# Where a reloaded tile lands, and two more places for x, in an adaLN attention and token-mixing kernel

## The chip, the cores and the metric

The kernel runs on one core of one Trainium2 chip. The metric is the device time of one execution in microseconds (us); lower is better. The kernel before was run three times: 2290.21, 2290.84 and 2291.17 us, median 2290.84. The profile is one further execution of it, which took 2293.52 us.

## The reference, cut to what matters

```
mod = (silu(c) @ w_mod)            # six rows: sa, ca, ga, sb, cb, gb
h = layernorm(x) * (1 + ca) + sa
x = x + ga * attention(h)          # 32 heads, 4 segments with a memory between them, then @ wo
h = layernorm(x) * (1 + cb) + sb
# token mixing: layernorm(h) once more, then two products across the 2048 tokens
u = gelu(einsum("bsd,sf->bdf", layernorm(h), w1) + b1)
x = x + gb * (einsum("bdf,fs->bds", u, w2) + b2).transpose
```

x has 2048 tokens of 1024 channels. The change lies between attention and mixing: the product with wo, the sum with x, and the two norms that follow.

## The kernel before, in words

The 2048 tokens are 16 tiles of 128. Attention runs over pieces (a group of four heads, a segment of 512 tokens) and writes its transposed output to oT in DRAM. The stage behind it, the one that the change touches, goes through the 16 token tiles in the order 0, 1, 8, 2, 9, 3, 10, 4, 11, 5, 12, 6, 13, 7, 14, 15. The mixing works on pairs (k, 8 + k): seven combinations of the halves of two tiles are its seven right operands, and its seven products q of a unit replace eight.

For each tile `product` does the following. L714 loads the attention output into otr. L122 and L125 (the helper `split`) make of it the two parts of ots on ScalarE and VectorE. L718 loads x into a tile x1. L729 runs 48 matmuls, 24 for each half of the channels, into two PSUM banks. L732, on VectorE, adds each half to x1 and leaves the bank free. L734 stores x1 to x1d in DRAM, where the end of the kernel needs it.

Then come three steps. `modulated`: the square of x1 on ScalarE (L703, L705, L706) with small VectorE steps (L707 to L709), and L754 and L755, which write the modulated norm into a tile h2; L754 is the last to read x1. `normed`: the square of h2 (L703 again, this time with mb), and L762, the second norm in place. `paired`, for the tiles from 8 on: L688 to L691 make the combinations. Pairs 0 to 2 are split into the operands bA on the spot; the others go to hcd in DRAM (L777 to L779) and come back later (L858).

The places: x1 has two, h2 has three, ots two, otr one. A place goes to the next tile of its name when all that read the last one are done. Tiles 2 and 3 are the EARLY ones: their products run just behind tile 1, while attention still works, since their tokens are complete by then. Their x1 is only stored; when their turn comes, `out_proj` takes a place of x1 again and reloads it from x1d (L744).

The mixing's first weights come by L803 in `prepare`, into a tile wr of 8 KB a partition, of which there are two places; s1, sp and bB are its other operands. Their memory is freed by the last product, wr's already by attention. In the kernel before, both places of wr are loaded when the stage begins.

All DMAs are issued by SyncE's queue (SPq), in one order. That order and the order on each engine come from the framework's scheduler, which takes the program's order for priority and a model of the times for what is ready; in the trace each engine, and SPq, goes through its own list in that order, so an instruction that waits stands before those behind it.

Of the kernel before, what the change touches and what calls it, by code (L numbers as in the profile page):

```python
# [2 lines left out]

# [4 lines left out]
F32 = mybir.dt.float32  # L8
# [9 lines left out]
S, D, H, DH, F = 2048, 1024, 32, 32, 3584  # L18
P = 128
# [27 lines left out]
def attention_and_mlp(ctx, tc, x, wq, wkv, wo, beta, w1, b1, w2, b2, c, wm_a, wm_b, out):  # L47
    nc = tc.nc
    V, A, G, T, SY = nc.vector, nc.scalar, nc.gpsimd, nc.tensor, nc.sync
# [4 lines left out]
    x1d = dram.tile([NT, P, D], F32, name="x1d")  # L54
# [12 lines left out]
    a = par.__enter__()  # L67
# [9 lines left out]
    def bank(tag, bufs, name):  # L77
        return psum.tile([P, 512], F32, tag=tag, bufs=bufs, name=name)
# [39 lines left out]
    def split(dst, src, hi_eng, lo_eng):  # L118

        hi, lo = dst[:, 0], dst[:, 1]  # L120
        if hi_eng is A:
            A.copy(hi, src)  # L122
        else:
            hi_eng.tensor_copy(hi, src)
        lo_eng.tensor_tensor(lo, src, hi.bitcast(F32), op=ALU.subtract)  # L125
# [177 lines left out]
    b = late.__enter__()  # L303
# [263 lines left out]
    def spread(dst, i):  # L567
        SY.dma_start(dst, bass.AP(tensor=modd.tensor, offset=modd.offset + D * i, ap=[[0, P], [1, D]]))
# [45 lines left out]
    for g in range(2, NG):  # L614
        n = 8 * g - 13
# [5 lines left out]
    for j in range(32):  # L621
        n = ML0 + MLS * j
        later(n, lambda j=j: mod_fetch(j), n + 2, lambda r, j=j: mod_late(j, r), "V")
    plan(WO0 - 3, lambda: spread(gaw, 0))
    for i in range(8):
        n = WO0 + WOS * i
# [30 lines left out]
    for q in skp + [late, prj, paw]:  # L657
# [6 lines left out]
    b3, raws, sx = (ctx.enter_context(tc.tile_pool(name=n, bufs=1, side="right", reuse_waits="tile"))  # L664
                    for n in ("b3", "wr", "s1"))
    cw_pool = tc.tile_pool(name="cw", bufs=1, side="right", reuse_waits="tile")
    w = cw_pool.__enter__()
# [18 lines left out]
    def t_combos(E, b11, b12, b21, b22, t):  # L686

        E.tensor_tensor(t[:, 0], b12, b11, op=ALU.subtract)  # L688
        E.tensor_tensor(t[:, 1], b22, t[:, 0], op=ALU.subtract)
        E.tensor_tensor(b12, b22, b12, op=ALU.subtract)  # L690
        E.tensor_tensor(t[:, 2], b21, t[:, 1], op=ALU.subtract)  # L691
# [7 lines left out]
    def rstd(src, nm, mv, sq):  # L699

        if sq is None:
            sq = wq_.tile([P, D], BF16, tag="sq", bufs=1, name="sq")
        A.activation(sq, src, AF.Square, bias=nm, accum_out=mv[:, 2:3])  # L703
        v, r0, t = mv[:, 0:1], mv[:, 1:2], mv[:, 2:3]
        A.activation(r0, t, AF.Ln, scale=1.0 / D, bias=eps)  # L705
        A.activation(r0, r0, AF.Exp, scale=-0.5)  # L706
        V.tensor_scalar(v, t, -0.5 / D, -0.5 * EPS, op0=ALU.mult, op1=ALU.add)  # L707
        V.tensor_scalar(t, v, r0, r0, op0=ALU.mult, op1=ALU.mult)
        V.tensor_scalar(r0, t, 1.5, r0, op0=ALU.add, op1=ALU.mult)  # L709

    def product(tt):

        r = wr_.tile([P, NK, P], F32, tag="otr", bufs=1, name=f"otr{tt}")
        SY.dma_start(r, oT[:, :, P * tt:P * tt + P].rearrange("g p n -> p g n"))  # L714
        os_ = ws_.tile([P, 2, D], F32R, tag="ots", bufs=2, name=f"ots{tt}")
        split(os_, r.rearrange("p a b -> p (a b)"), A, V)
        x1 = w.tile([P, D], F32, tag="x1", bufs=2, name=f"x1_{tt}")
        SY.dma_start(x1, x[P * tt:P * tt + P])  # L718
        ma = w.tile([P, 8], F32, tag="ma", bufs=2 + len(EARLY), name=f"ma{tt}")
        if tt == 0:  # L720
            for i in range(1, 3):
                gm[i] = w.tile([P, D], F32, name=f"gm{i}")
                spread(gm[i], i)
        for nh in range(2):
            ps = bank("pj", 2, f"po{tt}_{nh}")
            n = 0
            for ct in range(NK):
                for i, j in ((0, 0), (0, 1), (1, 0)):
                    T.matmul(ps, os_[:, i, P * ct:P * ct + P], wop[ct, nh][:, j], start=(n == 0), stop=(n == 3 * NK - 1))  # L729
                    n += 1  # L730
            c0, c1 = 512 * nh, 512 * nh + 512
            V.scalar_tensor_tensor(x1[:, c0:c1], ps, 1.0, x1[:, c0:c1], op0=ALU.mult, op1=ALU.add,  # L732
                                   accum_out=ma[:, 5 + nh:6 + nh])
        SY.dma_start(x1d[tt], x1)  # L734
        return x1, ma

    done = {}

    def out_proj(tt):

        if tt in done:
            ma = done[tt]
            x1 = w.tile([P, D], F32, tag="x1", bufs=2, name=f"x1r_{tt}")
            SY.dma_start(x1, x1d[tt])  # L744
        else:
            x1, ma = product(tt)
        h2 = w.tile([P, D], F32, tag="h2", bufs=3, name=f"h2_{tt}")
        mb = w.tile([P, 8], F32, tag="mb", bufs=2, name=f"mb{tt}")

        def modulated():  # L750
            nm = ma[:, 4:5]
            V.tensor_scalar(nm, ma[:, 5:6], ma[:, 6:7], -1.0 / D, op0=ALU.add, op1=ALU.mult)
            rstd(x1, nm, ma, h2 if tt == 15 else None)
            V.scalar_tensor_tensor(h2, x1, nm, gm[2], op0=ALU.add, op1=ALU.mult)  # L754
            V.scalar_tensor_tensor(h2, h2, ma[:, 1:2], gm[1], op0=ALU.mult, op1=ALU.add, accum_out=mb[:, 5:6])  # L755

        def normed():
            nm = mb[:, 4:5]
            V.tensor_scalar_mul(nm, mb[:, 5:6], -1.0 / D)
            rstd(h2, nm, mb, x1 if tt == 15 else None)  # L760
            V.tensor_scalar_mul(mb[:, 3:4], nm, mb[:, 1:2])
            A.activation(h2, h2, AF.Identity, scale=mb[:, 1:2], bias=mb[:, 3:4])  # L762

        def paired():
            if tt < 8:
                pair_h[tt] = h2
                return
            k = tt - 8
            first = pair_h.pop(k)
            t = w.tile([P, 3, 512], F32, tag="tc", bufs=1, name=f"tc{k}")  # L770
            t_combos(G if k == 7 else V, first[:, 0:512], first[:, 512:], h2[:, 0:512], h2[:, 512:], t)
            if k < 3:
                src = [first[:, 0:512], t[:, 0], t[:, 1], h2[:, 0:512], first[:, 512:], h2[:, 512:], t[:, 2]]
                for q in range(NPR):
                    split(bA[q][:, k], src[q], A, V)
            else:
                SY.dma_start(hcd[k, :, 0:2], first.rearrange("p (a n) -> p a n", a=2))  # L777
                SY.dma_start(hcd[k, :, 2:4], h2.rearrange("p (a n) -> p a n", a=2))
                SY.dma_start(hcd[k, :, 4:7], t)  # L779

        return modulated, normed, paired

    for tt in [0] + [i for k in range(1, 8) for i in (k, 7 + k)] + [15]:
        rest = out_proj(tt)
        if tt < 15:
            for f in rest:
                f()
        if tt == 1:
            for i in EARLY:
                done[i] = product(i)[1]  # L790
# [256 lines left out]
```

## Time and profile before

| | |
|---|---|
| median of 3 runs | 2290.84 us (2290.21 to 2291.17) |
| profiled execution | 2293.52 us |
| its span, first to last instruction | 2291.70 us |
| TensorE matmul, busy | 2214.7 us, 97% |
| VectorE, busy | 1677.2 us, 73% |
| ScalarE, busy | 1148.1 us, 50% |
| mean granted TensorE clock | 0.988 |

The span is 1.82 us less than the profiled execution's own time: that is what lies around it. Times inside the profile are us from the span's start. In the timeline a row gives start, length, engine, line, operation, output<-input and count, and in brackets the idle time before it with what ended it. In the list of waits a row gives who waited for whom, the sum in us, how often, and the longest. PE is TensorE, DVE VectorE, ACT ScalarE, POOL GpSimd, SPq SyncE's queue. The names x and h in the profile stand for x1 and h2 here (numbers are left out of names).

### The profile page before, as it was taken

The page shows a single profiled execution, that of the slowest core. Times are in us where ns is not written, and L with a number is a line of the kernel's source. Part 1 is how long each engine was busy: PE and PEld are TensorE (multiplying, and loading weights), DVE is VectorE, ACT ScalarE, POOL GpSimd, SP SyncE. Part 2 cuts the span into 40 slices and gives each one's busy share as a digit, 9 for nine tenths or more (in the row PEclk, how much of TensorE's full clock was granted, in tenths as well). Part 3 has the DMA queues.
Part 4 walks back from the last instruction along what each step waited for, and adds up shares of the span by engine and source line. Part 5 has one row for each costly group of instructions (what it writes and reads, how often), then busy time and mean ns, then how long its engine had stood idle before and what let it go on. Part 6 is the DMA issues. An engine that isn't in the chain of part 4 may idle for free.

```text
span 2291.7 us, 38412 instructions
## 1 busy us (share of the span) xinstructions
PE 2214.7 (97%) x13802; PEld 1903.6 (83%) x13802; DVE 1677.2 (73%) x3798; ACT 1148.1 (50%) x2090; POOL 733.1 (32%) x843
## 2 busy tenths in 40 slices
PE   7999999999999999999799999999999999999999
PEld 6888898888988889987687888888887888888887
DVE  6686677766776777664768565698889787878787
ACT  6476677664665666655555333443334242424232
POOL 5165566564766766644001000023333000000000
PEclk9999999999999999999999999999999999999999
DMA  6656565686566566673366664566557441414133
GB/s 258 201 169 180 144 198 162 180 280 218 165 192 207 169 196 182 202 250 107 114 218 243 238 238 164 192 230 237 207 202 264 173 152 55 152 56 143 55 120 147
DMA packets 172882, 415.72 MB, mean 181 GB/s; under 512 B 17268, under 2 KB 71572, under 8 KB 163732
## 3 DMA queue, kind: packets, MB, share of 16 engines
q1 hardware_dynamic: 172692, 413.27, 54.7%
q8 instruction: 110, 1.80, 0.3%
q14 instruction: 80, 0.66, 0.1%
HBM read 237.28 MB, written 125.06 MB: 158 GB/s over the span
## 4 chain that ended last, share of the span: by engine, by line
PE 77%; DVE 8%; DMA 6%; ACT 3%; POOL 3%; issue 2%; SPq 0%; DVEq 0%; ACTq 0%; POOLq 0%
PE mx L843 42%; PE nps L195 12%; PE qps L203 7%; PE po L729 4%; PE pv L503 3%; POOL ph L489 1%; PE a L474 1%; PE sx L439 1%; DVE ac L850 1%; PE sz L439 1%; DMA x<-in_x_dram 1%; DMA sk<-nt 1%; DVE sp L125 1%; PE rd L411 1%; PE a L477 1%
## 5 line engine op out<-in xcount | busy, mean ns | idle before, releaser
L843 PE MATMUL mx<-bU,sp 128*128 128x512 f32 x2352 | 535.8, 389 | 3.6 <-DVE sp L125 2.1
L843 PEld LDWEIGHTS mx<-bU,sp 128*128 128x128 f32 x2352 | 440.8, 188 | 98.1 <-DVE sp L125 3.2
L195 PE MATMUL nps<-wv,h 128*128 128x256 f32 x3072 | 435.8, 283 | 4.0 <-POOL h L125 3.9
L122 ACT CAST sp<-wr 128x384 fp32r<-128x384 f32 (+2 forms) x408 | 216.8, 545 | 439.4 <-PE mx L843 365.6
L843 PE MATMUL mx<-bA,sp 128*128 128x512 f32 x1764 | 431.5, 389 | 2.0 <-ACT sp L122 1.3
L489 POOL TENSOR_TENSOR ph<-p,ph 128x640 f16<-128x640 f32 x256 | 376.7, 1492 | 152.7 <-ACT ph L487 152.5
L195 PEld LDWEIGHTS nps<-wv,h 128*128 128x128 f32 x3072 | 403.6, 190 | 11.0 <-POOL h L125 5.0
L843 PEld LDWEIGHTS mx<-bA,sp 128*128 128x128 f32 x1764 | 330.8, 188 | 71.6 <-ACT sp L122 2.0
L125 DVE TENSOR_TENSOR sp<-wr,sp 128x384 fp32r<-128x384 f32 (+2 forms) x408 | 260.1, 649 | 31.9 <-ACT sp L122 31.5
L850 DVE TENSOR_TENSOR ac<-mx,ac 128x512 f32<-128x512 f32 x280 | 190.2, 688 | 91.7 <-PE mx L843 91.0
L203 PE MATMUL qps<-h,wq 128*128 128x512 f32 x768 | 200.3, 406 | 2.3 <-DVE pv L506 1.1
L729 PE MATMUL po<-wo,ots 128*128 128x512 f32 x768 | 185.9, 398 | 16.6 <-DVE x L732 14.5
L729 PEld LDWEIGHTS po<-wo,ots 128*128 128x128 f32 x768 | 145.5, 192 | 48.7 <-issue 9.7
L487 ACT CAST ph<-p 128x1280 f16<-128x1280 f32 x128 | 161.2, 1259 | 48.3 <-POOL p L485 47.6
L440 DVE CUSTOM_DVE_ANT_0 sx<-sx,mask 128x128 f32<-128x128 f32 (+1 forms) x256 | 110.1, 430 | 88.5 <-PE sx L439 87.1
L203 PEld LDWEIGHTS qps<-h,wq 128*128 128x128 f32 x768 | 144.1, 194 | 31.5 <-issue 2.8
L843 PE MATMUL mx<-bB,sp 128*128 128x512 f32 x588 | 164.6, 389 | 0.0
L485 POOL TENSOR_SCALAR_AFFINE_SELECT p<-p 128x256 f32<-128x256 f32 x256 | 120.5, 478 | 127.4 <-ACT p L478 68.2
L503 PE MATMUL pv<-vp,ph 128*128 128x97 bf16 (+1 forms) x2560 | 145.1, 203 | 3.3 <-DVE red L510 1.3
L503 PEld LDWEIGHTS <-ph 128*128 128x128 f16 x2560 | 115.9, 99 | 27.9 <-issue 13.1
L843 PEld LDWEIGHTS mx<-bB,sp 128*128 128x128 f32 x588 | 110.4, 188 | 22.9
L850 DVE TENSOR_TENSOR cc<-mx,cc 128x512 f32<-128x512 f32 x140 | 94.3, 684 | 42.5 <-PE mx L843 40.4
(201 smaller groups left out, 3209.2 us busy)
## 6 DMA issues: line engine op xcount, KB each, us to landing
sk<-sg SPq DMA_DIRECT2D x384, 128.0 KB
wr<-in_w_dram SPq DMA_DIRECT2D x28, 1024.0 KB
wr<-in_w_dram SPq DMA_DIRECT2D x32, 768.0 KB
bstu<-ucd SPq DMA_DIRECT2D x28, 768.0 KB
wsp<-wv SPq DMA_DIRECT2D x32, 512.0 KB
rawm<-in_wm_b_dram SPq DMA_DIRECT2D x32, 512.0 KB
wv<-wsp SPq DMA_DIRECT2D x32, 512.0 KB
pcd<-cc SPq DMA_DIRECT2D x14, 1024.0 KB
```

Of the source, the lines that this page charges most:

```text
L122: A.copy(hi, src)
L125: lo_eng.tensor_tensor(lo, src, hi.bitcast(F32), op=ALU.subtract)
L195: T.matmul(ps[:, aa], h[:, j, 128 * tt:128 * tt + 128], wt[:, i, o:o + 256], start=(n == 0), stop=(n >= 6 * NK - 2), skip_group_check=True)
L203: T.matmul(ps, wt[:, i, o:o + 128], h[:, j], start=(k + n == 0), stop=(3 * k + n == 3 * NK - 1))
L440: marks[4 * t + h - LEADS, "V"] = V.tensor_tensor_reduce(o, o, mask[:, 384 - 128 * i:], 1.0, -3.0e38, op0=ALU.add, op1=ALU.max, accum_out= ...
L485: G.affine_select(w, w, pattern=[[0, 2], [1, 128]], compare_op=ALU.is_ge, fill=0.0, base=0, channel_multiplier=-1)
L487: marks[n, "A"] = A.copy(ph[:, 0], p32)
L489: marks[n, "G"] = G.tensor_tensor(ph[:, 1, c], p32[:, c], ph[:, 0, c], op=ALU.subtract)
L503: T.matmul(pv[:, i, 0:w], ph[:, part, o:o + 128], d["vp"][:, j, h, 0:w], start=(n == 0), stop=(n == 19), skip_group_check=True)
L729: T.matmul(ps, os_[:, i, P * ct:P * ct + P], wop[ct, nh][:, j], start=(n == 0), stop=(n == 3 * NK - 1))
L843: T.matmul(ps, ops[q][:, i, P * k:P * k + P], b[:, j], start=(m == 0 and first), stop=(m == 3 * nk - 1), skip_group_check=True)
L850: V.tensor_tensor(d, ps, d, op=ALU.add)
```

## The change

The reloaded x1 of tiles 2 and 3 no longer takes a place of x1: it is loaded into the tile's own h2, where L754 then overwrites it. And of every four products' x1, the first two go into the two halves of a new tile `more_x1`, which takes one of the two places of wr before the first weights do; the other two go to the two places of x1 as before. So x1 has four places, and the second of the mixing's weight tiles can be loaded only when all of `more_x1` is done with.

```diff
+import itertools
...
-        x1 = w.tile([P, D], F32, tag="x1", bufs=2, name=f"x1_{tt}")
+        n_x1 = next(count)
+        if n_x1 % 4 < 2:
+            x1 = more_x1[:, n_x1 % 4]
+        else:
+            x1 = w.tile([P, D], F32, tag="x1", bufs=2, name=f"x1_{tt}")
         SY.dma_start(x1, x[P * tt:P * tt + P])
...
     done = {}
+    count = itertools.count()
+    more_x1 = raws.tile([P, 4, 512], F32, tag="wr", bufs=2, name="more_x1").rearrange("p (a b) n -> p a (b n)", a=2)
...
-        if tt in done:
-            ma = done[tt]
-            x1 = w.tile([P, D], F32, tag="x1", bufs=2, name=f"x1r_{tt}")
-            SY.dma_start(x1, x1d[tt])
-        else:
+        if tt not in done:
             x1, ma = product(tt)
         h2 = w.tile([P, D], F32, tag="h2", bufs=3, name=f"h2_{tt}")
+        if tt in done:
+            x1, ma = h2, done[tt]
+            SY.dma_start(x1, x1d[tt])
```

## The prediction

> **What bounds the kernel now.** I read the page first, then the list of waits between 985 and 1230 us, then the timeline engine by engine. The page:
>
> ```profile
> PE 2214.7 (97%) x13802; PEld 1903.6 (83%) x13802; DVE 1677.2 (73%) x3798; ACT 1148.1 (50%) x2090; POOL 733.1 (32%) x843
> L729 PE MATMUL po<-wo,ots 128*128 128x512 f32 x768 | 185.9, 398 | 16.6 <-DVE x L732 14.5
> ```
>
> TensorE is busy for 97% of the span, so only its idle time is to be had, and what delays it in one stage shifts all that follows. The second row is the product with wo: 16.6 us idle before its matmuls, 14.5 of it ended by L732, which adds x and frees the bank. The waits, DVE's and PE's first, then SPq's:
>
> ```profile
> PE po L729 <- DVE x L732: 14.5, 5, 9.3
> DVE x L732 <- DMA x<-in_x_dram: 9.5, 6, 2.3
> ...
> SPq L718 <- DVE h L754: 19.2, 6, 10.3
> ...
> SPq L718 <- ACT ma L705: 11.7, 5, 4.4
> ```
>
> Read downwards this is one chain: the product waits for the sum, the sum for the load of x, and the load (L718) for the norm of an earlier tile, L754 and the square before L705, to give up its place. TensorE's timeline shows where:
>
> ```profile
> 1076.47 20.70 PE L729 MATMUL po<-wo,ots 128*128 128x512 f32 x90
> 1106.44 13.80 PE L729 MATMUL po<-wo,ots 128*128 128x512 f32 x48 [9.27 <-DVE x L732]
> 1121.99 22.02 PE L729 MATMUL po<-wo,ots 128*128 128x512 f32 x96 [1.76 <-DVE x L732]
> 1145.53 22.01 PE L729 MATMUL po<-wo,ots 128*128 128x512 f32 x96 [1.52 <-DVE x L732]
> 1169.03 43.80 PE L729 MATMUL po<-wo,ots 128*128 128x512 f32 x192 [1.49 <-DVE x L732]
> 1214.14 2.87 PE L843 MATMUL mx<-bA,sp 128*128 128x512 f32 x11 [1.31 <-ACT sp L122]
> ```
>
> The last row is the mixing's start. The big hole is 9.27 us, before tile 4: tile 10's two banks are full and its x isn't there. Why, by SPq, DVE and ACT (a fence each), and the chain of work that ended last:
>
> ```profile
> 1057.32 0.32 SPq L744 DMA_DIRECT2D x1r<-x1d  x1
> ...
> 1094.33 0.32 SPq L744 DMA_DIRECT2D x1r<-x1d  x1
> 1099.54 0.37 SPq L714 DMA_DIRECT2D otr<-oT  x1
> 1100.88 0.33 SPq L718 DMA_DIRECT2D x<-in_x_dram  x1
> ```
>
> ```profile
> 1093.02 1.28 DVE L754 SCALAR_TENSOR_TENSOR h<-x1r,ma,gm 128x1024 f32<-128x1024 f32 x1
> 1094.21 1.28 DVE L754 SCALAR_TENSOR_TENSOR h<-x,ma,gm 128x1024 f32<-128x1024 f32 x1
> ```
>
> ```profile
> 1099.63 1.13 ACT L703 ACTIVATE sq<-x,ma 128x1024 bf16<-128x1024 f32 x1
> ```
>
> ```profile
> 1100.88 4.69 DMA x<-in_x_dram
> ```
>
> Tile 2's reload takes one of the two places at 1057.32 and holds it, doing nothing, until L754 at 1093.02, when pair (0, 8) has left an h2. Tile 9's x holds the other until its square at 1099.63 ends, 1100.76. At 1100.88 tile 10's load goes out, and takes 4.69 us.
>
> **The change part by part.**
>
> *Two more places, none for reloads.* Product n of the order now takes the place of product n-4. The stores of tile 3's x1 and L754 of tiles 4 and 11 in the kernel before, on SPq and DVE, and what one product of 48 matmuls takes, in the chain:
>
> ```profile
> 1054.53 0.33 SPq L734 DMA_DIRECT2D x1d<-x  x1
> ```
>
> ```profile
> 1139.87 2.48 DVE L754 SCALAR_TENSOR_TENSOR h<-x,ma,gm 128x1024 f32<-128x1024 f32 x2
> ```
>
> ```profile
> 1121.99 11.16 PE po L729 x48
> ```
>
> Tile 10 takes the place of tile 2, tile 4 that of tile 3, whose store went out at 1054.53: both are free before tile 8's product. Tile 11 takes that of tile 8, tile 5 that of tile 9, free at 1100.76 at the latest. At 11.16 us a product from 1097 on (tile 10's old end), tiles 4, 11, 5, 12, 6 start near 1097, 1108, 1119, 1130 and 1142, and the first sum of each is due 5.6 us later. The tightest is tile 6 in the place of tile 4: even at its old time L754 is through at 1142.4, the load lands at 1147, the sum is due at 1147 and TensorE stops for it only a half product later. So four of the five holes that L732 ends should close (the fifth, 0.5 us, is tile 0's): 9.27 + 1.76 + 1.52 + 1.49 = 14.04 us.
>
> The clock comes on top. Behind the big hole 48 matmuls took 13.80 us, against 11.16. That is 2.64 us, and the granted clock in that stretch says the same (the third number from the end):
>
> ```profile
> 1061.00:1097.00 36.00, 35.90 (x174) 29.12 (x174) 24.93 (x49) 15.62 (x28) 4.00 (x5) 0.95 0.39 124
> 1097.00:1122.00 25.00, 13.97 (x50) 10.88 (x49) 17.88 (x44) 14.81 (x27) 0.00 (x0) 0.80 0.27 85
> 1169.00:1190.00 21.00, 20.97 (x92) 17.38 (x93) 14.88 (x38) 9.57 (x19) 0.00 (x0) 1.00 0.67 229
> 1214.00:1236.00 22.00, 21.19 (x92) 17.07 (x93) 21.55 (x41) 15.22 (x30) 1.29 (x1) 1.00 0.59 216
> ```
>
> [...]
>
> So 14.04 + 2.64 = 16.7 us. A second way gives the other bound, from the first matmuls of tile 8 and attention's last among them:
>
> ```profile
> 1061.10 2.08 PE L729 MATMUL po<-wo,ots 128*128 128x512 f32 x4 [1.02 <-ACT ots L122]
> ...
> 1069.12 0.92 PE L503 MATMUL pv<-vp,ph 128*128 128x97 bf16 x20
> ...
> 1076.12 0.60 PE L518 MATMUL ops<-ident,am 128*128 128x128 f32 x4
> ```
>
> Twelve products of 11.16 us and 1.5 us of attention's would end at 1061.1 + 133.9 + 1.5 = 1196.5; the clock of 0.95 over the first 36 us adds about 1 that stays (it lies before the hole), 1197.5. They ended at 1169.03 + 43.80 = 1212.8. That is 15.3 us. I take **16 us off**.
>
> *The first loads into wr's memory.* Tiles 0 and 1 now land there, at a place that attention must have left:
>
> ```profile
> 1001.78 0.36 SPq L718 DMA_DIRECT2D x<-in_x_dram  x1
> ...
> 1003.90 0.94 SPq L803 DMA_DIRECT2D wr<-in_w_dram  x2
> ```
>
> wr was loaded 2.1 us behind tile 0's x, so the place is free at 1003.90 at the latest; earlier isn't shown. The cost lies between 0 and 2.1 us, on a product that attention's own matmuls surround; I take 0.5, near the lower end. The second load of wr, 1 MB, leaves this crowded spot: a gain that I count as nothing.
>
> *The reload into h2.* It has the same one DMA, but it can be issued only when pair (0, 8) gives up an h2, about 1093 (L754 above, the first to use the place). At 4.69 us for the load and 1.13 for the square, tile 2's L754 comes near 1099 instead of 1093, tile 3's likewise some 6 us behind its old order. Neither is on TensorE's path: tile 2 is needed with tile 10, whose L754 stood right behind tile 3's, 20 us later:
>
> ```profile
> 1116.22 1.28 DVE L754 SCALAR_TENSOR_TENSOR h<-x1r,ma,gm 128x1024 f32<-128x1024 f32 x1
> ...
> 1118.02 1.28 DVE L754 SCALAR_TENSOR_TENSOR h<-x,ma,gm 128x1024 f32<-128x1024 f32 x1
> ```
>
> Cost 0 with that cover; 6 us of the norms' time, not TensorE's, without it. On ScalarE the square of tile 2 no longer stands before that of tile 9, so tile 9's norm may come up to 5 us sooner.
>
> *What is late next.* The products now run ahead of the norms. The norms go in rounds of one pair, since h2 has three places; L754 of tile 7 and of tile 14, on DVE:
>
> ```profile
> 1201.59 1.28 DVE L754 SCALAR_TENSOR_TENSOR h<-x,ma,gm 128x1024 f32<-128x1024 f32 x1 [0.83 <-DMA hcd<-h]
> ...
> 1204.85 1.28 DVE L754 SCALAR_TENSOR_TENSOR h<-x,ma,gm 128x1024 f32<-128x1024 f32 x1
> ...
> 1210.26 1.28 DVE L755 SCALAR_TENSOR_TENSOR h<-h,ma,gm 128x1024 f32<-128x1024 f32 x1
> ...
> 1216.99 0.69 DVE L813 TENSOR_TENSOR s<-wr 128x512 f32<-128x512 f32 x1
> ```
>
> From tile 10's L754 to tile 14's, four rounds, it was 86.8 us, 21.7 each, against 22.3 for two products: they keep pace, but the 16 us are not made up. If the rounds come 8 us earlier, half of it, L754 and L755 of tile 14, L755 of tile 7 and some ten small steps of 0.2 us still stand before VectorE when the mixing starts: 3 x 1.28 + 2 = 5.8 us. In the stretch from 1214 VectorE was busy 21.55 of 22 us, so nothing hides them there. A matmul group of the mixing needs a split only every 12 matmuls (2.7 us), which VectorE makes in 0.7: it catches up. The cost lies between 0 and 5.8 us; I take 3, the middle.
>
> *The second unit's weights.* The wr tile that L813 reads at 1216.99 can now be loaded only when tiles 13 and 7, the last two in `more_x1`, are through L754. That is 1202.9 at the latest by the row above. With 1 MB at twice the bytes of the load of 4.69 us, at most 9.4 us, it lands by 1212.3. The mixing starts near 1198, and its first unit alone has 84 matmuls of 0.23 us, 19 us: the second unit's first operand is due near 1217. Cost 0, with 4 us to spare; if L754 comes later than 1207, its lateness is the cost.
>
> *The sum*: -16 + 0.5 + 3 = **-12.5 us**. Made against the profiled execution: 2293.52 - 12.5 = 2281.0. The median of the runs is 2.68 us below that execution, so I forecast 2290.84 - 12.5 = **2278.3 us**.
>
> **The rivals.**
>
> *A: the weights, or VectorE, take back half.* Head of SPq: if the load of the second unit's weights is issued as soon as the scheduler thinks its place free, and waits there, the reloads of pair 3 (bsth) behind it wait too, with the mixing's bB. Price: from 1198 to 1203, 5 us, plus the upper end of the backlog, 5.8 instead of 3: the gain falls to about 5 us, 2286. For it: VectorE at 98% in that stretch. Against it: 63 of a unit's 84 matmuls need no bB.
>
> *B: given back, no change.* The products end earlier and wait for the norms, at 2290. It holds if x1's places still depend on a norm that is late, for instance if the two halves of `more_x1` were one thing to the framework: tile 5's load would wait for tile 11's L754 (about 1134, due 1125) and tile 7's for tile 13's. Against it is that halves of one tile are followed apart already, on PE and POOL:
>
> ```profile
> 1058.21 1.00 PE L503 MATMUL pv<-vp,ph 128*128 128x97 bf16 x10 [1.13 <-ACT ph L487]
> ```
>
> ```profile
> 1058.23 2.75 POOL L489 TENSOR_TENSOR ph<-p,ph 128x640 f16<-128x640 f32 x2 [0.27 <-ACT ph L487]
> ```
>
> L503 reads the first half of ph while GpSimd still writes the second.
>
> *C: slower, SPq's head.* The reload now waits for a pair, in a queue that goes in order. Behind it stand the loads of otr, without which a product can't start. If tile 3's reload is placed ahead of the load of otr for tile 11 (due about 1101: 4.69 us to land and 2.3 to be split before 1108), SPq stands until pair (1, 9) is through: tile 3's old L754 came about 23 us behind tile 2's, at 1116.22, and 4.69 + 2.3 us later the product starts, 1123 instead of 1108: 15 us lost. Tile 2's reload ahead of otr for tile 4 costs 5 more in the same way, with 2.6 for the clock. Sum: 15 + 5 + 2.6 - 12.5 = +10, **2301 us**. It turns slower from 12.5 us of lost product time on. For it: SPq already stood 10.3 us before one L718. Against it: otr for those tiles went out at or before 1099.54, well ahead of pair (1, 9).
>
> [...]
>
> **How the numbers follow.** Forecast 0.60; A 0.14; B 0.09; C 0.17. The forecast's own range is 2273 (16.7 us, and 1 of the noise between runs) to 2284 (backlog 5.8, place 2.1, and 16.7 less 2). The whole range, with A and the edge of B, is 2272 to 2290: it leaves out most of C and a little of B. 0.2% of the time, 4.6 us, is about what a measurement of this kernel can tell from no change. Faster by more than that, under 2286.3: the forecast and most of A, 0.72. Within it: the rest of A, B, a mild C, 0.13. Slower: C, 0.15.
>
> **What would show it.** Right: no hole of over 2 us before L729 from 1076 on; clock 1.00 from 1097 to 1122; L718 for tile 10 issued before 1061; L744 near 1093 and 1115; the first L843 near 1198; L803 for the second unit behind tile 7's L754 and landed before 1212. Wrong: L729 waiting for ots or otr (C); L843 waiting for sp or bB in its first 40 us for more than 3 us in sum (A); holes before L729 that L732 ends, with loads behind a norm (B). The forecast fails too if attention's tail, which shares all queues until 1061, is drawn out by the new order.

## The result, and the profile after

The changed kernel takes 2302.66 us, the median of five runs (2300.01 to 2304.07); the kernel before took 2290.84 us beside it (2289.0 to 2294.16). The ratio is 1.0049, 95% interval 1.0036 to 1.0063: half a percent slower, where 2278.3 us and a gain were forecast, and the time lies above the whole range. The profiled execution took 2302.72 us, its span is 2300.9 us, 9.2 us more than before. (That the medians lie 11.8 us apart and the spans 9.2 comes from the profiled execution of before, which lay 2.7 us above its median.) One execution of the kernel with five places for h2, below, took 4876.91 us; the ratio given there leaves it out, the median does not (without it, 2284.1).

The page of after has the product's row and a row of the mixing, its 588 matmuls with bB. The columns after the bar are busy time, mean of one, and idle time before them with what ended most of it:

```profile
PE 2215.7 (96%) x13802; PEld 1903.6 (83%) x13802; DVE 1676.5 (73%) x3798; ACT 1149.5 (50%) x2090; POOL 736.8 (32%) x843
...
L734 PE MATMUL po<-wo,ots 128*128 128x512 f32 x768 | 183.9, 396 | 6.3 <-DVE more_x L737 3.1
...
L849 PE MATMUL mx<-bB,sp 128*128 128x512 f32 x588 | 165.7, 392 | 18.6 <-ACT bB L123 18.0
```

The product's 16.6 us of idle time have become 6.3, and another row has 18.6 instead. TensorE's timeline shows when:

```profile
1081.12 89.22 PE L734 MATMUL po<-wo,ots 128*128 128x512 f32 x392
1172.62 22.01 PE L734 MATMUL po<-wo,ots 128*128 128x512 f32 x96 [2.28 <-DVE more_x L737]
1195.55 4.97 PE L849 MATMUL mx<-bA,sp 128*128 128x512 f32 x20 [0.92 <-ACT sp L123]
1200.72 1.88 PE L849 MATMUL mx<-bA,sp 128*128 128x512 f32 x7 [0.21 <-DVE sp L126]
1220.02 0.80 PE L849 MATMUL mx<-bB,sp 128*128 128x512 f32 x1 [17.41 <-ACT bB L123]
```

The products run without a hole from 1081 to 1170, and the mixing starts at 1195.55 instead of 1214.14: 18.6 us earlier. Of these, 2.0 us were there when the stage began, since in these two profiles the first matmul of the product starts at 986.9 and 988.9; the other 16.6 us were won in the stage. Then 20 + 7 matmuls with bA are done, and TensorE stands for 17.41 us until the first piece of bB has been cast. What the cast waited for, on SPq and on ScalarE in after:

```profile
1205.09 1.65 SPq L809 DMA_DIRECT2D wr<-in_w_dram  x2
1216.65 0.33 SPq L864 DMA_DIRECT2D bsth<-hcd  x1
```

```profile
1215.38 1.15 ACT L704 ACTIVATE sq<-h,mb 128x1024 bf16<-128x1024 f32 x1 [0.40 <-DVE mb L765]
1216.44 0.19 ACT L704 ACTIVATION_READ_ACCUMULATOR sq<-h,mb 128x1 f32 x1
```

The load of bB's staging tile (bsth) goes out 0.02 us after the read behind tile 14's second-norm square has ended, at 1216.63. They have no data in common. They have memory in common: in the built program sq, the scratch that each square writes, and bsth lie at the same byte (87776) of a partition. The same pair in the kernel before, on ScalarE and SPq, and SPq's own waits there:

```profile
1211.78 1.15 ACT L703 ACTIVATE sq<-h,mb 128x1024 bf16<-128x1024 f32 x1 [0.40 <-DVE mb L759]
1212.83 0.19 ACT L703 ACTIVATION_READ_ACCUMULATOR sq<-h,mb 128x1 f32 x1
```

```profile
1213.04 0.32 SPq L858 DMA_DIRECT2D bsth<-hcd  x1
```

```profile
SPq L858 <- ACT mb L705: 9.2, 1, 9.2
```

The wait was there already. It ended at 1213.02, and the last product, by the prediction's own rows, at 1212.8. Two chains ended within 0.2 us of each other. Only the products showed holes: while the first piece of bB was loaded and cast, TensorE had 11 matmuls with bA to do, and its first with bB started at 1216.85 without a gap. The change shortened one of the two chains.

The other, the norms, did not merely stay: it became longer. L760 reads x1 and writes h2; these rows are of after, on DVE, with the reloads on SPq:

```profile
1115.91 1.28 DVE L760 SCALAR_TENSOR_TENSOR h<-x,ma,gm 128x1024 f32<-128x1024 f32 x1
1119.64 1.27 DVE L760 SCALAR_TENSOR_TENSOR h<-h,ma,gm 128x1024 f32<-128x1024 f32 x1
...
1142.56 1.27 DVE L760 SCALAR_TENSOR_TENSOR h<-x,ma,gm 128x1024 f32<-128x1024 f32 x1
```

```profile
1088.86 0.32 SPq L753 DMA_DIRECT2D h<-x1d  x1
...
1114.21 0.32 SPq L753 DMA_DIRECT2D h<-x1d  x1
```

`h<-h` is the reloaded tile 3. Its load can't go out before 1114.21, when a pair has left its h2, so its L760 comes at 1119.64, where the kernel before, with its x waiting in a place, had it at 1116.22. The next round starts at 1142.56 instead of 1139.87, and the square that sets bB free ends 3.6 us later than before, though the products end 18 us earlier.

Most of the rest of the loss is the clock. For L843 (before) and L849 (after) alone, the columns are length, TensorE busy and matmuls, granted clock, DMA share, GB/s; the first row is of before, the others of after:

```profile
1190.00:1350.00 160.00, 135.19 (x595) 1.00 0.63 234
```

```profile
1190.00:1350.00 160.00, 132.79 (x552) 0.91 0.62 225
```

```profile
1206.00:1210.00 4.00, 0.00 (x0) 0.50 0.97 330
...
1223.00:1226.00 3.00, 2.22 (x5) 0.50 0.93 348
1226.00:1229.00 3.00, 3.00 (x8) 0.50 0.34 90
1229.00:1232.00 3.00, 3.00 (x14) 0.94 0.30 70
```

The account closes with these. From its first matmul to 1350 the mixing of after had 1350 - 1195.55 = 154.45 us, was busy for 132.79 and so idle for 21.7; at the 135.19 / 595 = 0.227 us of before, 552 matmuls take 125.4 us, so in after they took 7.4 us longer. Of these an estimated 5.5 us are the clock's: the mixing was busy for 7.23 us at a granted 0.50 from 1220 to 1229, for 1.00 us at 0.82 up to 1230, and for 4.00 us at a mean of 0.57 from 1236 to 1240; at the full clock the same work would have taken 3.6, 0.2 and 1.7 us less. What the other 1.9 us are was not shown. Before, 0.7 us were idle. So 18.6 ahead, 21.7 + 7.4 - 0.7 = 28.4 lost: 9.8 us behind at 1350, against 9.2 at the end of the span.

### The profile page after: what moved, and what is told of

Its sections match the earlier page's. It is cut to its first block, busy times and chain, and to the rows that moved or that the text cites. A ratio compares the mean times of both kernels' runs of the same rounds, so it can differ in the third digit from the quotient of the medians.

```text
span 2300.9 us, 38398 instructions
## 1 busy us (share of the span) xinstructions
PE 2215.7 (96%) x13802; PEld 1903.6 (83%) x13802; DVE 1676.5 (73%) x3798; ACT 1149.5 (50%) x2090; POOL 736.8 (32%) x843
## 4 chain that ended last, share of the span: by engine, by line
PE 79%; DMA 7%; DVE 6%; ACT 3%; POOL 2%; issue 2%; SPq 0%; DVEq 0%; ACTq 0%; POOLq 0%
PE mx L849 41%; PE nps L196 13%; PE qps L204 7%; PE po L734 6%; PE pv L504 3%; PE a L475 1%; PE sx L440 1%; DMA xb<-x1d 1%; POOL ph L490 1%; PE sz L440 1%; DMA x1e<-xb 1%; PE rd L412 1%; DMA sk<-nt 1%; PE a L478 1%; DMA more_x<-in_x_dram 1%
## 5 line engine op out<-in xcount | busy, mean ns | idle before, releaser
L849 PE MATMUL mx<-bU,sp 128*128 128x512 f32 x2352 | 535.4, 389 | 3.5 <-DVE sp L126 1.7
L849 PEld LDWEIGHTS mx<-bU,sp 128*128 128x128 f32 x2352 | 440.9, 188 | 97.5 <-DVE sp L126 2.7
L849 PE MATMUL mx<-bA,sp 128*128 128x512 f32 x1764 | 435.8, 392 | 4.0 <-ACT cc L854 1.6
L849 PEld LDWEIGHTS mx<-bA,sp 128*128 128x128 f32 x1764 | 333.3, 189 | 76.7 <-ACT cc L854 2.7
L849 PE MATMUL mx<-bB,sp 128*128 128x512 f32 x588 | 165.7, 392 | 18.6 <-ACT bB L123 18.0
L849 PEld LDWEIGHTS mx<-bB,sp 128*128 128x128 f32 x588 | 110.6, 189 | 43.0 <-ACT bB L123 18.8
L689 POOL TENSOR_TENSOR tu<-cc 128x512 f32<-128x512 f32 x14 | 22.8, 1630 | 344.6 <-DVE cc L985 283.6
```

What stands on the lines that cost most here:

```text
L849: T.matmul(ps, ops[q][:, i, P * k:P * k + P], b[:, j], start=(m == 0 and first), stop=(m == 3 * nk - 1), skip_group_check=True)
```

## Experiments

Theory N: the norms, which go in rounds through the three places of h2, set when bB may be loaded, through the memory of sq; what the products win is worth nothing until that wait is gone, and the reload into h2 makes the rounds longer. Rival W: the second unit's weights, which now have no place of their own before the products are through, hold the mixing. In three of the last four, rival S puts the loss down to ScalarE's order, whatever place is freed.

**The scratch moved, in the kernel after.** bsth then lies over ots, which the last product frees.

```diff
-    ot_pools = [tc.tile_pool(name=n, bufs=1, reuse_waits="tile") for n in ("otr", "ots", "sq")]
-    wr_, ws_, wq_ = (q.__enter__() for q in ot_pools)
+    ot_pools = [tc.tile_pool(name=n, bufs=1, reuse_waits="tile") for n in ("otr", "sq", "ots")]
+    wr_, wq_, ws_ = (q.__enter__() for q in ot_pools)
```

> The changed kernel with one thing undone: the scratch tile sq of the norms lies between otr and ots in memory, so that bsth (the reloads of pair 3 for the mixing) no longer lies over it, but over ots. Theory N (the norms: bsth's first load waits for the last square written to sq, that of tile 14's second norm, and that hid behind the products before): the first L864 goes out within 2 us of the last product's end, near 1196 instead of 1216.65; the hole of 17.4 us before bB goes, and with it some 3 to 5 us of half clock: 2279 to 2286 us. Theory W (the second unit's weights in the place of more_x1, and their load ahead of bsth in the queue): bsth still goes out behind the loads of wr at 1205, the hole shrinks by 5 us at most: 2296 or more.

2288.62 us, ratio to before 0.9988 (0.9979 to 0.9998): 14 us faster than the changed kernel, from an edit that moves 2 KB of scratch and alters no instruction, though the scheduler puts some in another order. bsth goes out at 1192.73 and no longer waits for a square. The mixing starts at 1193.57, 2.0 us earlier than in after, so up to 2 of the 14 us can be the order's. Of W this remains:

```profile
1201.07 1.14 PE L849 MATMUL mx<-bB,sp 128*128 128x512 f32 x3
1211.07 4.21 PE L849 MATMUL mx<-bA,sp 128*128 128x512 f32 x9 [8.86 <-ACT sp L123]
```

```profile
1203.51 0.38 SPq L809 DMA_DIRECT2D wr<-in_w_dram  x1
```

```profile
1210.40 0.62 ACT L123 CAST sp<-wr 128x512 fp32r<-128x512 f32 x1 [5.52 <-DMA wr<-in_w_dram]
```

(TensorE, SPq, ScalarE.) The first unit now has bB from 1197.86 on, and the hole of 8.86 us waits for the second unit's weights: their load goes out at 1203.51, where in before it went out at 1003.90, and their first cast ends at 1211.02. N is the main cause; W was a second wait behind it, 2.6 us above the edge of what N gave.

**The same edit in the kernel before.**

> The kernel before with the same move of sq. Theory N: the last product's end (1212.83) and the last square on sq (1213.02) coincide there, so the move frees nothing: within 0.2% of the kernel before, first L858 at 1212.9. A rival, that the move of memory alone is worth time (other neighbours, another schedule), expects a gain of the same size as in the changed kernel.

2292.82 us, ratio 1.0005 (0.9994 to 1.0016): no change. bsth goes out at 1215.24, since there the products, which now free its memory, end at 1215.2. The wait costs only once the products are ahead.

**The reload alone**, into h2, in the kernel before, with x1 left at two places.

```diff
-        if tt in done:
-            ma = done[tt]
-            x1 = w.tile([P, D], F32, tag="x1", bufs=2, name=f"x1r_{tt}")
-            SY.dma_start(x1, x1d[tt])
-        else:
+        if tt not in done:
             x1, ma = product(tt)
         h2 = w.tile([P, D], F32, tag="h2", bufs=3, name=f"h2_{tt}")
+        if tt in done:
+            x1, ma = h2, done[tt]
+            SY.dma_start(x1, x1d[tt])
```

> Only the first part of the change: the reload of tiles 2 and 3 goes into h2; x1 keeps two places and wr both of its own. Theory N: the products end earlier by part of the 9.3 us hole, but the last square on sq comes at 1213 to 1217, and the mixing's bB with it: 2289 to 2296 us, no gain. Theory R (the reload's latency lengthens the rounds of the norms, and that alone is the loss): 3 to 4 us slower than before, 2294 to 2296. Theory W: no loss, since the weights keep their place: 2284 to 2291.

2302.94 us, ratio 1.0055 (1.004 to 1.007): slower by 12 us, more than any theory gave. The hole didn't close, it moved, and grew (TensorE, then SPq):

```profile
1133.91 13.46 PE L729 MATMUL po<-wo,ots 128*128 128x512 f32 x48 [13.28 <-DVE x L732]
```

```profile
1117.90 0.32 SPq L746 DMA_DIRECT2D h<-x1d  x1
1123.00 0.37 SPq L714 DMA_DIRECT2D otr<-oT  x1
1129.55 0.33 SPq L718 DMA_DIRECT2D x<-in_x_dram  x1
```

The load of x for tile 11 goes out only at 1129.55. It needs the place of an x1 whose square (here the last to read it, and not L754) stands, in ScalarE's order, behind that of tile 3, which was reloaded at 1117.90. So by these rows the late reload holds up the products as well, and both chains end late: the mixing starts at 1219.94, bsth goes out at 1219.46.

**The places alone**: `more_x1` for the products and for the reloads, none into h2.

```diff
-        x1 = w.tile([P, D], F32, tag="x1", bufs=2, name=f"x1_{tt}")
+        n_x1 = next(count)
+        if n_x1 % 4 < 2:
+            x1 = more_x1[:, n_x1 % 4]
+        else:
+            x1 = w.tile([P, D], F32, tag="x1", bufs=2, name=f"x1_{tt}")
```

> Only the second part: two places more for x in wr's memory; tiles 2 and 3 are reloaded into places of x1 as before. Theory N: the products end about 10 to 15 us earlier, the last square on sq comes near its old time, 1211 to 1214, and bB with it: a hole of 8 to 14 us, cold clock behind it: 2293 to 2299. Theory R: without the reload's latency the loss is gone: 2290 or less. Theory W: the loss stays whole, 2300 to 2304.

2293.24 us, ratio 1.0009 (0.9998 to 1.0019). This can't be told from before. N's range holds it, but not by N's way, since the products didn't end earlier: in the profile (of an execution of 2299.36 us) two holes of 4.43 and 9.32 us before the product remain, the mixing starts at 1214.69, and bsth goes out at 1216.47. Twice as many places for x1, and nothing won: a reloaded tile still sits in one, waiting for an h2. The x whose load goes out at 1118.86 takes the place that the reloaded tile 3 left with its L761 at 1118.78.

**The scratch moved and a place of its own for the second unit's weights**, in after. The weights go to one of the three places of `cc`, in which the mixing's results lie and which is free then.

```diff
-        r = raws.tile([P, 4, 512], F32, tag="wr", bufs=2, name="wr")[:, :, 0:n]
+        pool, tag, bufs = place or (raws, "wr", 2)
+        r = pool.tile([P, 4, 512], F32, tag=tag, bufs=bufs, name="wr")[:, :, 0:n]
...
-            unit = prepare(w1[units[u + 1]], 4)
+            unit = prepare(w1[units[u + 1]], 4, (cp, "cc", 3) if u == 0 else None)
```

> The changed kernel with sq moved as in after_sq_moved, and the second unit's weights loaded into one of the three places of cc (free at the last product's end) in place of wr. In after_sq_moved TensorE stood 8.86 us for these weights, which could be loaded only at 1203.51. Theory N with W as a second wait behind it: that hole and the cold clock behind it go, about 11 us: 2275 to 2280 us. If something else of the norms is next (VectorE's order), the hole only moves and the time stays at 2285 to 2290.

2292.76 us, ratio 0.9999 (0.9987 to 1.0011): the expected gain didn't come. TensorE has the hole again, SPq and ScalarE show why:

```profile
1217.91 2.08 PE L850 MATMUL mx<-bB,sp 128*128 128x512 f32 x3 [13.39 <-ACT bB L123]
```

```profile
1205.83 0.38 SPq L810 DMA_DIRECT2D wr<-in_w_dram  x1
...
1207.95 0.42 SPq L865 DMA_DIRECT2D bsth<-hcd  x1
1209.82 0.33 SPq L810 DMA_DIRECT2D wr<-in_w_dram  x1
...
1219.11 0.43 SPq L810 DMA_DIRECT2D wr<-in_w_dram  x1
```

```profile
1211.34 1.15 ACT L704 ACTIVATE sq<-h,mb 128x1024 bf16<-128x1024 f32 x1 [4.23 <-DVE mb L765]
...
1216.11 1.24 ACT L768 ACTIVATE h<-h,mb 128x1024 f32<-128x1024 f32 x1 [1.50 <-DVE mb L767]
1217.26 0.60 ACT L123 CAST bB<-bsth 128x512 fp32r<-128x512 f32 x1
```

The fourth piece of bB was asked for at 1207.95, but its cast stands on ScalarE behind steps of the norms' last rounds, which themselves wait for VectorE. So, by these rows, the norms hold bB in a second way: by the order of ScalarE, where before it was by memory. And the new place did not bring the weights forward. In the built program's list for SPq the loads at 1205.83 and 1209.82 are those of the third and fourth unit, and the second unit's weights, with no wait of their own, stand behind them and go out only at 1219.11. So W's wait was not taken away here, and it could be seen only if the hole for bB were gone.

**Two controls.** The weights' place alone, in after, and both edits in before:

> The changed kernel with only the second unit's weights in a place of cc; sq where it was. Theory N: bsth still waits for tile 14's last square on sq, near 1216, so little comes back: 2297 to 2303 us. Theory W alone as the cause: the loss goes, 2291 or less.

> The kernel before with both edits, as a control. Its products end at 1213, when the norms are nearly through, and its weights have lain in their place since 1004. Nothing to gain: 2289 to 2294. A gain as large as in after_sq_weights would mean that the edits help by themselves and the change adds nothing.

2297.36 us, ratio 1.0023 (1.0014 to 1.0032), with the first wait untouched (`17.02 <-ACT bB`), and 2291.66 us, 0.9996 (0.9985 to 1.0007). W as the only cause is refuted, though the edit is worth about 5 us in after (1.0023 against 1.0049), by a way that no run shows. The kernel before gets nothing from both edits together; there the second one delays the second unit's weights from 1003.90 to 1221.93.

**Both edits with the places alone**, that is the change without the reload into h2:

> The two places for x alone (reloads into places of x1 as before), with both edits. In places_alone the products still had holes of 4.4 and 9.3 us and ended at 1214, so there is little for the edits to set free: 2286 to 2292 us. If instead the reload into h2 is only a loss (it lengthens the norms' rounds), this is the fastest of all, 2272 to 2278.

2287.26 us, ratio 0.9979 (0.997 to 0.9989), inside the first of the two. In the profile the mixing has no hole over 0.6 us in its first 50, but the products have holes again, of 1.55 us and the one shown:

```profile
1115.16 89.71 PE L734 MATMUL po<-wo,ots 128*128 128x512 f32 x384 [11.33 <-DVE x L737]
1205.38 4.44 PE L851 MATMUL mx<-bA,sp 128*128 128x512 f32 x18 [0.51 <-ACT sp L123]
```

A hole for x without the reload into h2, a hole for bB with it: by the order of the rows, what both wait for is an h2. Here the load of x goes out at 1109.82, right behind the L761 that frees its place, that of the reloaded tile 3 (1108.51 to 1109.79).

**The same memory given to h2.** x1 keeps two places, the reload stays where it was, h2 has five.

```diff
-        h2 = w.tile([P, D], F32, tag="h2", bufs=3, name=f"h2_{tt}")
+        n_h2 = next(count) % 5
+        if n_h2 < 2 and tt < 15:
+            h2 = more_h2[:, n_h2]
+        else:
+            h2 = w.tile([P, D], F32, tag="h2", bufs=3, name=f"h2_{tt}")
...
+    count = iter(range(16))
+    more_h2 = raws.tile([P, 4, 512], F32, tag="wr", bufs=2, name="more_h2").rearrange("p (a b) n -> p a (b n)", a=2)
```

> The kernel before with the other use of the same memory: the two places taken from the mixing's weights go to h2 (five places in all), x1 keeps its two, the reload stays in a place of x1. Theory N (rounds): what holds both the places of x1 and the mixing's first operands is the serial rounds of the norms, which wait for pairs to give up an h2; with five places L754 no longer waits, so holes before the product fall under 4 us in sum, the square of tile 14's second norm ends before 1206, the mixing starts near 1200, and only the second unit's weights (their place is free when tile 6's h2 has been stored) take a few us back: 2279 to 2288. Rival S (order): whatever is freed ahead of the mixing is lost behind it, since the casts for bB stand behind the norms in ScalarE's order: 2288 to 2294, with a hole of 8 us or more in the mixing's first 25 us.

2284.91 us, ratio 0.9954 (0.9939 to 0.9968): 0.46% faster than before by the ratio, without moving the scratch. TensorE, ScalarE and SPq:

```profile
1101.04 23.53 PE L729 MATMUL po<-wo,ots 128*128 128x512 f32 x96 [2.75 <-DVE x L732]
1124.90 76.41 PE L729 MATMUL po<-wo,ots 128*128 128x512 f32 x336 [0.33 <-DVE x L732]
```

```profile
1196.48 1.15 ACT L703 ACTIVATE sq<-h,mb 128x1024 bf16<-128x1024 f32 x1 [3.22 <-DVE mb L765]
```

```profile
1197.74 0.32 SPq L864 DMA_DIRECT2D bsth<-hcd  x1
```

x1 still has two places, yet the hole of 9.27 us is 2.75. The last square before bB ends at 1197.7 instead of 1213.0, and bsth goes out with it. N said so; S expected 8 us of hole in the mixing, and its longest is 1.3 us.

**With both edits, and with the place divided** between x1 (three places) and h2 (four), first with the reload as before, then with it in h2:

```diff
-        x1 = w.tile([P, D], F32, tag="x1", bufs=2, name=f"x1_{tt}")
+        x1 = more[:, 0] if next(n_x1) % 3 == 0 else w.tile([P, D], F32, tag="x1", bufs=2, name=f"x1_{tt}")
...
-        h2 = w.tile([P, D], F32, tag="h2", bufs=3, name=f"h2_{tt}")
+        h2 = more[:, 1] if next(n_h2) % 4 == 0 else w.tile([P, D], F32, tag="h2", bufs=3, name=f"h2_{tt}")
```

> The same with the scratch of the squares moved and the second unit's weights in a place of cc. Theory N: 2275 to 2282, no hole over 3 us from 1100 to 1240. Rival S: 2285 to 2292, with a hole of 8 us or more before a matmul of the mixing that waits for the cast of bB.

> The kernel before with the place of the weights halved: three places for x1, four for h2; the reload as before, the scratch moved, the second unit's weights in a place of cc. Theory N: 2276 to 2284; it has both fewer pairs to wait for and a place more for x. Rival S: 2285 to 2292.

> The kernel named last, with tiles 2 and 3 reloaded into their own h2. Theory N: the reload now has a fourth h2 to land in, so it costs less than the 5 to 6 us that it cost with three places (2292.76 against 2287.26 with the four places for x1): 0 to 3 us above the kernel named last. If the reload into h2 costs by itself, wherever it lands, 5 us or more above it.

The first gives 2284.48 us, 0.9965 (0.9949 to 0.9981), above what N gave, and no gain on five places of h2 alone. S's hole isn't there either (the longest in the mixing's first 50 us is 1.07 us); what keeps this kernel at that time is open. The second gives 2279.28 us, 0.9938 (0.9915 to 0.996), the third 2278.74 us, 0.9932 (0.9905 to 0.9959); before took 2293.06 us in these runs. Both beat before, by 0.6 to 0.7%, and by the ratios the changed kernel by 1.1%. With a fourth h2 to land in, the reload costs nothing that can be measured, where with three it stood beside a loss of 5.5 us (2292.76 against 2287.26; the late load of the weights may have a part in that). In the two kernels with the divided place the second unit's weights go out at 1201.52 and 1206.17. In the second one TensorE has one hole of over 1 us left among the products from 1070 on, and the mixing starts at 1196.63:

```profile
1140.54 56.25 PE L729 MATMUL po<-wo,ots 128*128 128x512 f32 x240 [3.92 <-DVE x L732]
...
1198.19 2.34 PE L846 MATMUL mx<-bA,sp 128*128 128x512 f32 x9 [0.94 <-DVE sp L125]
```

```profile
1190.00:1350.00 160.00, 151.65 (x660) 1.00 0.66 241
```

That last row is the mixing's again: 660 matmuls by 1350, where before had done 595 and after 552, at the full clock.

## Why the prediction was wrong, point by point

- *Two more places, 16 us off.* Right: 16.6 us were won up to the mixing's start, besides the 2.0 that were there before. Three of the four holes are gone, and one of 2.28 us is left. It is tile 7's: its x (L723 in after) went out at 1165.12, right behind the L760 that freed its place (1163.78 to 1165.07), so not every load found its place free. The second way of counting gave an end of 1197.5 for the products, against 1194.6, 2.0 of which are the earlier start.
- *The first loads into wr's memory, 0.5 us.* Nothing of it is seen: the first x goes out at 999.51, and wr follows at 1003.16, as early as before.
- *The reload into h2, cost 0.* Wrong. Its working saw that tile 3's L754 would come later and called that "6 us of the norms' time, not TensorE's". The norms' time was TensorE's time, a hundred microseconds further on. Alone it costs 12 us; what it costs within the change was not measured by itself.
- *What is late next, 3 us.* **The step that failed.** It asked how much of VectorE's backlog would stand before the mixing, and took the norms' lateness only as that. It didn't ask for each operand of the mixing when its memory comes free. The text ahead of the prediction says that the memory of bB and the others is "freed by the last product"; for bB's staging tile that is not so, and the list of waits of before had the row for it, SPq's 9.2 us for `ACT mb`. In place of 3 us stand 17.41 us of hole and, behind it, an estimated 5.5 us of slower clock. With the old rounds the square would have ended 3.6 us sooner, which by an estimate (17.41 - 3.6) leaves a hole of some 14 us.
- *The second unit's weights, cost 0, with 4 us to spare.* Wrong, but hidden: the hole for bB lies over it in after. With the scratch moved, it shows as 8.86 us. The place was misjudged: the load at 1203.51 goes out ahead of the last L760 that reads `more_x1`, at 1206.13, so it took the place of the first unit's own weights. So was the due time: 1217 counted 84 matmuls of the first unit in a row, but TensorE stood for the second unit's first operand after some 33.
- *Rival A* had the right operand and the wrong reason. Against it stood "63 of a unit's 84 matmuls need no bB". By the trace only 27 went ahead: TensorE's matmuls go in the order of its list, in which three nines with bA stood ahead of the first matmul with bB.
- *Rival B* had the norms as what takes the gain back, but at the products, through the places of x1. The wait came one stage later, at bB.
- *Rival C* gave 2301 us, close to the time, by a mechanism that did not occur: SPq stood 9.2 us before the two L753, but no product behind them lost time. A price that fits is no support for its cause.
- *What would show it.* The signs named for the products came true but for one (the hole of 2.28 us, where none of over 2 was to be): tile 10's x went out early, L753 at 1088.86 and 1114.21, and the mixing started at 1195.55. The one that spoke was "L843 waiting for sp or bB in its first 40 us for more than 3 us in sum": it was 17 us and more.

What the runs show: moving the scratch is worth 14 us in after and nothing in before; more places of h2 shorten both chains at once. What is only argued, from the order of the rows: that the 12 us of the reload alone come from ScalarE's order of squares, and that the hole in the kernel with both edits comes from its order of casts. Both lie in the order that the scheduler chose, and no run changed that order alone; every edit changed it along with the memory.

## What to carry to other kernels

When a hole on the bounding engine is to be closed, list what the next stage waits for, operand by operand, with the memory each is loaded into and who used it last, and compare those times with the new start, not with the old; a wait that ends as close to the hole's end as the 0.2 us here is a candidate for the next bound. If two chains end together, look for the one resource that both wait for (here the three places of h2) before giving memory to either. And a wait for memory between tiles with no data in common can go by changing the order of allocation, but it gains only where it shows (14 us in after, nothing in before).

## What the runs showed of the hardware

The clock was dearer than expected. In the prediction a hole of 9.27 us cost 2.64 us behind it. Here the granted clock was 0.50 from 1206 to 1229, 9 us beyond the first matmul behind the hole, while TensorE worked with gaps of 0.43 and 1.32 us among its first 14 matmuls. It was 0.94 from 1229 to 1232 and fell to 0.50 once more (from 1237 to 1239), and the loss to the clock, by the estimate above, was 5.5 us in sum. TensorE worked without a gap from 1223.78, and 5.2 us of that, up to 1229, were at 0.50. Behind the hole of before, with steady work from 1106.44, it was 5.6 us (TensorE in before, columns as above):

```profile
1111.00:1112.00 1.00, 1.00 (x4) 0.50 0.00 0
1112.00:1113.00 1.00, 1.00 (x5) 0.97 0.00 0
```

So in these two cases the steady work at the half clock was about as long, 5.2 and 5.6 us. What came on top behind the second hole were the gaps, which put off the steady work by 3.8 us (1220.02 to 1223.78), and the second fall of the clock. No run varied these gaps alone, so what set the clock's return was not shown.
